# Transformer block on one core: head masks moved from K to Q, two heads' scores in one matmul, units of eight heads for the narrow token tiles

## The chip, the cores and the metric

The kernel runs on one core of a Trainium2 chip. The metric is device time in microseconds of one execution, the median of several runs; lower is better. The profile is one execution recorded by the hardware profiler. Its span runs from the first to the last instruction; the execution's own time is a little longer.

## The reference, cut to what matters

```python
x = A_x                                   # (1, 2048, 512), bf16
h = layernorm(x) * (1 + ca) + sa          # sa, ca, ga, sb, cb, gb from silu(c) @ w_mod
q, k, v = split(h @ wqkv)                 # 32 heads of 16 columns
p = softmax(q @ k.T * 16 ** -0.5)         # per head, 2048 x 2048
x = x + ga * (concat(p @ v) @ wo)
h = layernorm(x) * (1 + cb) + sb
x = x + gb * ((gelu(h @ w_gate) * (h @ w_up)) @ w_down)     # width 1792
```

Each head has only 16 columns, so the 32 x 2048 x 2048 exponentials weigh more than the matmuls.

## The kernel before, in words

**Layout.** Q and K lie transposed: 128 partitions hold a chunk of eight heads, and there are four chunks (`dc`). A row group of 32 partitions (`j`) holds two heads, an even and an odd one. A score matmul contracts over the 32 partitions of one row group, so one of its operands must have the other head's 16 rows at zero. Before, that is K: it is kept twice, `kme` with the odd heads zeroed and `kmo` with the even ones, written from one projection by two passes with a mask column each (`side_k`, L786 to L794). Q is kept once, scaled (`side_q`, L796). V is kept with a column of ones per head (`vaug`), so that the product with the exponentials also gives the softmax's denominator.

**Sets, units, rounds, banks.** Tokens of Q are worked in seven sets (`SETS`, L29): two of 512 tokens, three of 256 and two of 128. A unit is one set and one `qd` from 0 to 7, which means four heads, one in each row group: the even or the odd heads of chunk `qd // 2`. For `qd` 0 and 1 the last two sets share a unit of 256 tokens. Scores go into PSUM banks of 512 columns (`ps_sc`). A bank holds one head's scores of 512 / W key tiles for W tokens, and takes as many matmuls (`qk`, L1559): one for W = 512, two for 256, four for 128. A round is four banks, one for each head of the unit. A unit has 16 rounds at W = 512, 8 at 256 and 4 at 128. A *position* is one bank in the order of the work; there are 2048, and sets 5 and 6 begin at position 1792. PSUM has eight banks: six for scores (and now and then side work), `ps_pv` for the running products with V, and `ps_mi` for side work.

**Exponentials.** ScalarE (ACT) takes two or three banks in one exp (L403) and writes bf16 into the ring `E`. VectorE (DVE) takes some banks: from each bank a pass to an integer with the exponent in its upper bits (`bits`, L1329), and for every *quad* (the four banks of one round) three passes over 2048 columns, `mant`, `square` and `expo` (L1600 to L1614), which give two bf16 factors whose sum of products replaces the exponential. A quad holds two of ten buffers (`bufs`, L552) while it lasts. Two of these buffers are also the staging room of streamed feed-forward weights: `spare` (L1587) keeps quads out of them from shortly before the first feed-forward on, to the end (`closing`, L1450). A round may become a quad only if it is not one of its unit's last three (`cand`, L1291, with `LAST = 3`), and if it is still far enough ahead (`ahead`).

**End of a unit.** `unit_end` (L1629) copies the sums out of `ps_pv`, sends the denominators through two small DRAM scratch tensors to spread them over partitions, takes reciprocals, broadcasts them back by four DMAs, and multiplies into `onorm`. For a few late units (`PEN`, L34) it uses 32 x 32 transposes on DVE instead of the DMAs.

**Side work.** Projections, the output projection, layer norm and the feed-forward of finished sets run beside attention in small steps that a planner issues. The feed-forward of sets 0 to 3 streams its weights through staging buffers; that of sets 4 to 6 uses weights that are resident by then (`weight_parts`, L923): gate weights in Q's memory of finished tokens, down weights in `xs`, up weights in the staging buffers and a weight region. Ten parts are loaded early, from 8 positions after the end of set 3, and eleven after set 3's feed-forward. Side matmuls are split into four of 32 output rows each, so that they run in the same mode as the products with V; those of set 4's gate and up projections are kept whole, in groups of four (`WUP`, `JOIN`, L63).

**Order.** `stream` (L1242) writes the whole program at build time. At each step it looks at its own model of the engines' free times and chooses among scores, products with V, side work and filler matmuls (which keep PE's activity up). `RULES` (L73) gives nine thresholds of that choice for each stretch of 64 positions: among them `back` (backlog of DVE steps), `fill` (wanted PE activity) and `ahead`. Each engine executes its instructions in the order written; SP issues nearly all DMAs.

Of the kernel before, what the change touches and what calls it, by code (L numbers as in the profile page):

```python
# [7 lines left out]
ALU = mybir.AluOpType  # L8
# [25 lines left out]
PEN = {NSET - 2: (6, 7), NSET - 1: (5, 6, 7)}  # L34
# [18 lines left out]
def WIN(ends):  # L53
# [9 lines left out]
WUP, WDOWN, WWO, JOIN = (4,), (), (), 4  # L63
# [442 lines left out]
class _Kernel(_Recorder):  # L506
# [12 lines left out]
    def alloc(self):  # L519
        sb, ps = self.sb, self.ps  # L520
        self.xs = sb("xs", [P, NT, D], BF16)
        self.qT = sb("qT", [P, NDC, S_TOK], BF16)
        self.km = [sb("kme", [P, NDC, S_TOK], BF16), sb("kmo", [P, NDC, S_TOK], BF16)]
# [22 lines left out]
        self.wg = [self.qT[:, :, 256 * i:256 * i + 256] for i in range(6)]  # L546
        self.wg.append(hreg[:, NFC * 256:NFC * 256 + 1024].rearrange("p (a n) -> p a n", a=NDC))
        self.wu = [self.wst[i // 2][i % 2] for i in range(4)]
        self.wu += [dreg[:, 1024 * i:1024 * i + 1024].rearrange("p (a n) -> p a n", a=NDC) for i in range(4, 7)]
# [43 lines left out]
    def prologue(self):  # L593
# [27 lines left out]
        self.memset(pool, self.rm4, 1.0)  # L621
# [3 lines left out]
        self.ts(dve, self.rm[:, 0:1], self.rm[:, 1:2], -1.0, 1.0, ALU.mult, ALU.add)  # L625
# [39 lines left out]
        qb = [self.scp[:, 0, 0:256], self.scp[:, 1, 0:256]]  # L665
# [10 lines left out]
        self.act(self.km[0][:, 0, ks[0]], kb[0], ACT.Copy, scale=self.rm[:, 0:1])  # L676
        self.ts(dve, self.qT[:, 0, 0:256], qb[0], Q_SCALE, None, ALU.mult)
        self.act(self.qT[:, 0, 256:512], qb[1], ACT.Copy, scale=Q_SCALE)
        for i, h in ((0, 1), (1, 0), (1, 1)):
            self.ts(dve, self.km[i][:, 0, ks[h]], kb[h], self.rm[:, i:i + 1], None, ALU.mult)  # L680
# [61 lines left out]
    def proj(self, bank, col, g):  # L742
        for dci in range(NDC):
            self.mm(bank, self.wqkv[:, dci, col:col + P], self.hT[:, dci, 512 * g:512 * g + 512],
                    start=(dci == 0), stop=(dci == NDC - 1))
# [1106 lines left out]
```

## Time and profile before

| | |
|---|---|
| median of 3 runs | 816.21 us (816.03 to 817.04) |
| profiled execution | 815.63 us |
| its span | 813.9 us, 29942 instructions |
| DMA | 43.70 MB, mean 54 GB/s |
| granted TensorE clock | 1.000 |

In a row of groups stand: line, engine, operation, output and inputs by the program's names, output shape and input shape, count; then busy time in us and the mean duration of one in ns; then idle time of the engine just before them and who ended it. For matmuls, `32*128 32x256` means 32 contraction rows by 128 output rows, moving 256 columns. Since every operation is recorded by a helper, most lines are those of helpers: L384 is a matmul, L403 an ACT instruction, L407 a DVE product or sum of two tensors, L415 a DVE pass with a scalar, L424 a copy, L427 a reciprocal. In a row of the timeline stand the start, the length and the merged instructions with their count. In a row of waits stand who waited for whom, the total in us, the times and the longest.

### The profile page before, as it was taken

How to read it: one execution, taken by the hardware profiler on the slowest of the kernel's cores; microseconds unless marked ns; L12 is line 12 of the kernel's file. 1: busy time of each engine (PE TensorE's matmuls, PEld its weight loads, DVE VectorE, ACT ScalarE, POOL GpSimd, SP SyncE). 2: the span in 40 equal slices, each digit the busy share in tenths (PEclk: the TensorE clock that was granted, in tenths of full speed). 3: DMA queues.
4: the chain of work that ended last, by engine and by line, in shares of the span. 5: the costliest groups of instructions: out<-in, count | busy, mean ns of one | idle time of the engine just before them, and what ended most of it. 6: DMA issues, size and time to landing. Idle time of an engine off the chain costs nothing.

```text
span 813.9 us, 29942 instructions
## 1 busy us (share of the span) xinstructions
PE 749.1 (92%) x13549; PEld 301.0 (37%) x13549; DVE 753.3 (93%) x1369; ACT 792.0 (97%) x742; POOL 4.6 (1%) x13
## 2 busy tenths in 40 slices
PE   8999999888998988899998999999999999999998
PEld 3333332322222222222233333333553345456566
DVE  7877999999999999999999999999999999788675
ACT  6999999999999999999999999999999999999993
POOL 2000000000000000000000000000000000000000
PEclk9999999999999999999999999999999999999999
DMA  9100000000002211110003212100554243241000
GB/s 286 52 16 23 10 11 9 10 9 10 2 10 64 83 48 35 46 45 20 16 18 98 62 49 58 55 26 12 163 151 126 63 113 88 59 120 40 20 9 15
DMA packets 77354, 43.70 MB, mean 54 GB/s; under 512 B 21285, under 2 KB 75626, under 8 KB 77226
## 3 DMA queue, kind: packets, MB, share of 16 engines
q1 hardware_dynamic: 77224, 41.78, 18.6%
q8 instruction: 106, 1.74, 0.9%
q14 instruction: 22, 0.18, 0.1%
q10 hardware_dynamic: 2, 0.00, 0.0%
HBM read 39.15 MB, written 2.60 MB: 51 GB/s over the span
## 4 chain that ended last, share of the span: by engine, by line
ACT 84%; PE 8%; DVE 7%; DMA 0%; issue 0%; DVEq 0%
ACT E L403 80%; PE ps_sc L384 4%; ACT hreg L403 2%; PE ps_mi L384 2%; ACT L403 1%; DVE mreg L415 1%; PE ps_pv L384 1%; DVE dreg L415 1%; DVE st L446 1%; DVE mreg L407 1%; DVE hreg L415 0%; DMA xs<-in_A_x_dram 0%; DVE hreg L424 0%; PE ps_mi L388 0%; DVE mv L449 0%
## 5 line engine op out<-in xcount | busy, mean ns | idle before, releaser
L403 ACT ACTIVATE E<-ps_sc 128x1024 bf16<-128x1024 f32 (+1 forms) x701 | 746.0, 1301 | 3.0 <-PE ps_sc L384 2.8
L384 PE MATMUL ps_sc<-qT,kmo 32*128 32x256 bf16 (+2 forms) x1728 | 199.0, 294 | 23.2 <-ACT E L403 20.2
L384 PE MATMUL ps_sc<-qT,kme 32*128 32x256 bf16 (+2 forms) x1728 | 196.5, 294 | 22.0 <-ACT E L403 18.0
L415 DVE TENSOR_SCALAR mreg<-ps_sc 128x512 uint16<-128x512 f32 x256 | 171.6, 684 | 9.0 <-PE ps_sc L384 6.6
L384 PE MATMUL ps_pv<-E,vaug 128*17 128x256 bf16 (+2 forms) x2720 | 148.7, 291 | 0.2
L384 PEld LDWEIGHTS ps_sc<-qT,kme 32*128 32x128 bf16 x1728 | 57.9, 92 | 143.0 <-ACT E L403 125.5
L384 PE MATMUL ps_mi<-wreg,mreg 128*32 128x512 bf16 (+2 forms) x1792 | 106.6, 329 | 3.6 <-DVE hreg L407 1.2
L415 DVE TENSOR_SCALAR dreg<-ps_sc 128x512 uint16<-128x512 f32 x156 | 103.6, 684 | 4.9 <-PE ps_sc L384 3.6
L384 PEld LDWEIGHTS ps_sc<-qT,kmo 32*128 32x128 bf16 x1728 | 58.4, 92 | 128.8 <-ACT E L403 113.0
L384 PEld LDWEIGHTS ps_pv<-E,vaug 128*17 128x17 bf16 x2720 | 53.7, 89 | 55.6 <-issue 40.9
L415 DVE TENSOR_SCALAR mreg<-mreg 128x2048 uint16<-128x2048 uint16 x102 | 69.0, 681 | 0.1
L384 PEld LDWEIGHTS ps_mi<-wreg,mreg 128*32 128x32 bf16 (+1 forms) x1792 | 40.5, 95 | 44.0 <-issue 19.6
L384 PE MATMUL ps_pv<-mreg,vaug 128*17 128x256 bf16 (+2 forms) x848 | 50.0, 298 | 3.5 <-DVE mreg L407 1.9
L407 DVE TENSOR_TENSOR mreg<-mreg 128x2048 bf16<-128x2048 bf16 x38 | 46.1, 1214 | 0.1
L384 PE MATMUL ps_mi<-hreg,wreg 128*32 128x512 bf16 x480 | 39.5, 385 | 0.9 <-DVE qT L415 0.5
L407 DVE TENSOR_TENSOR mreg<-dreg,mreg 128x2048 bf16<-128x2048 bf16 x32 | 38.6, 1210 | 0.0
L424 DVE CAST hreg<-ps_mi 128x512 bf16<-128x512 f32 x49 | 33.6, 685 | 2.3 <-PE ps_mi L384 1.9
L384 PE MATMUL ps_mi<-wo,onorm 128*32 128x512 bf16 x416 | 31.6, 384 | 0.5 <-DVE onorm L407 0.5
L407 DVE TENSOR_TENSOR hreg<-ps_mi,hreg 128x512 bf16<-128x512 f32 x45 | 30.8, 684 | 1.3 <-PE ps_mi L384 1.0
L407 DVE TENSOR_TENSOR dreg<-mreg,dreg 128x2048 bf16<-128x2048 bf16 x26 | 31.5, 1212 | 0.0
L415 DVE TENSOR_SCALAR dreg<-dreg 128x2048 uint16<-128x2048 uint16 x46 | 31.1, 677 | 0.0
L384 PE MATMUL ps_pv<-xs,nil 128*17 128x512 bf16 (+1 forms) x464 | 30.3, 339 | 0.0
(167 smaller groups left out, 681.4 us busy)
## 6 DMA issues: line engine op xcount, KB each, us to landing
mreg<-in_B_w_up_dram SPq DMA_DIRECT2D x32, 256.0 KB, 2.9
mreg<-in_B_w_gate_dram SPq DMA_DIRECT2D x28, 256.0 KB, 3.1
mreg<-in_B_w_down_dram SPq DMA_DIRECT2D x16, 256.0 KB, 2.8
dreg<-in_B_w_down_dram SPq DMA_DIRECT2D x12, 256.0 KB, 5.3
mreg<-in_w_mod_dram SPq DMA_DIRECT2D x1, 2048.0 KB, 12.2
rb<-scr_rec SPq DMA_DIRECT2D x64, 32.0 KB, 1.9
out_dram<-xs SPq DMA_DIRECT2D x15, 128.0 KB, 1.8
rb<-scr_rec SPq DMA_DIRECT2D x104, 16.0 KB, 1.9
```

The source lines that it names most:

```text
L384: return self.rec("pe", lambda e: e.matmul(out, lhsT, rhs, start=start, stop=stop, tile_position=tp), [lhsT, rhs, *after], [out], cost=(n, ...
L403: return self.rec("act", lambda e: e.activation(out, in_, func, scale=scale, **kw), rd, wr, cost=self.cost("act", out, [in_], "act") + load)
L407: return self.rec(eng, lambda e: e.tensor_tensor(out, a, b, op), [a, b], [out], cost=self.cost(eng, out, [a, b], "tt"))
L415: return self.rec(eng, lambda e: e.tensor_scalar(out, a, s1, s2, **kw), rd, [out], cost=self.cost(eng, out, [a], "ts") + (60 if len(rd) > ...
L424: return self.rec(eng, lambda e: e.tensor_copy(out, in_), [in_], [out], cost=self.cost(eng, out, [in_], "ts"))
L446: return self.rec("dve", lambda e: e.bn_stats(out, in_), [in_], [out], cost=self.cost("dve", out, [in_], "bn"))
```

## The change: what it does, and the diff

- K is kept once (`kT`), Q twice (`qT[:, 0]` for even heads, `qT[:, 1]` for odd heads), with mask and scale in one column `rm`. A K chunk is one plain copy, a Q chunk two passes.
- From set 2 on, a unit is two `qd` (eight heads), with `n = 2`. Its score matmul has one row group of `kT` as weights and moves the even and the odd Q side by side: 2 x 256 columns for 256 tokens (one matmul per bank, not two), 2 x 128 for 128 tokens (two, not four). A bank now holds both heads' scores for half as many key tiles. The last two `qd` of set 6 stay apart (`APART`), with four heads each and four matmuls per bank.
- A unit of 256 tokens thus has 16 rounds, one of 128 tokens eight, and the joint unit 16. Products with V keep their number and width, but those of the two heads go into different columns of the one `ps_pv` bank. Before the first of a paired unit, four matmuls with zero weights clear the bank.
- `unit_end` works on the wider unit, with one chain of small DMAs for eight heads. `PEN` is set anew.
- Up weights for the resident feed-forward go into the odd half of Q's memory. Eighteen parts are loaded early (after set 1's feed-forward as well) and three late. The staging buffers are given back to quads once set 3's feed-forward is done, and only streaming feed-forwards wait for them.
- Set 4's gate and up matmuls are no longer whole (`WUP` is empty).
- 30 of the 32 rows of `RULES` have other thresholds. Three unused projection functions are removed.

```diff
-PEN = {NSET - 2: (6, 7), NSET - 1: (5, 6, 7)}
+PEN = {NSET - 2: (6,), NSET - 1: (4, 6, 7)}
+APART = {NSET - 2: (), NSET - 1: (6, 7)}
-WUP, WDOWN, WWO, JOIN = (4,), (), (), 4
+WUP, WDOWN, WWO, JOIN = (), (), (), 4
...
-        self.qT = sb("qT", [P, NDC, S_TOK], BF16)
-        self.km = [sb("kme", [P, NDC, S_TOK], BF16), sb("kmo", [P, NDC, S_TOK], BF16)]
+        self.qT = sb("qT", [P, 2, NDC, S_TOK], BF16)
+        self.kT = sb("kT", [P, NDC, S_TOK], BF16)
-        self.wg = [self.qT[:, :, 256 * i:256 * i + 256] for i in range(6)]
+        self.wg, self.wu = ([self.qT[:, x, :, 256 * i:256 * i + 256] for i in range(6)] for x in range(2))
...
         def fin(mi):
-            self.ts("dve", self.km[0][:, dc, sl], mi, self.rm[:, 0:1], None, ALU.mult)
-            self.ts("dve", self.km[1][:, dc, sl], mi, self.rm[:, 1:2], None, ALU.mult)
+            self.copy("dve", self.kT[:, dc, sl], mi)
...
         def fin(mi):
-            self.ts("dve", self.qT[:, dc, 512 * g:512 * g + 512], mi, Q_SCALE, None, ALU.mult)
+            for e in range(2):
+                self.ts("dve", self.qT[:, e, dc, 512 * g:512 * g + 512], mi, self.rm[:, e:e + 1], None, ALU.mult)
...
-        return g[:6] + d[:4], g[6:] + u + d[4:]
+        return g + u[:6] + d[6:] + d[:4], u[6:] + d[4:6]
...
-        while not self.dry and self.held & {1, 2}:
+        while flow and not self.dry and self.held & {1, 2}:
...
-        units = [((k,), qd) + SETS[k] for k in range(NSET - 2) for qd in range(8)]
-        units += [((NSET - 2, NSET - 1), qd, SETS[NSET - 2][0], 2 * P) for qd in range(QS)]
-        units += [((k,), qd) + SETS[k] for k in (NSET - 2, NSET - 1) for qd in range(QS, 8)]
+        units = [((k,), qd) + SETS[k] + (1,) for k in range(2) for qd in range(8)]
+        units += [((k,), qd, SETS[k][0], 2 * SETS[k][1], 2) for k in range(2, NSET - 2) for qd in range(0, 8, 2)]
+        units += [((NSET - 2, NSET - 1), qd, SETS[NSET - 2][0], 4 * P, 2) for qd in range(0, QS, 2)]
+        for k in (NSET - 2, NSET - 1):
+            units += [((k,), qd, SETS[k][0], 2 * P, 2) for qd in range(QS, 8, 2) if qd not in APART[k]]
+            units += [((k,), qd, SETS[k][0], P, 1) for qd in APART[k]]
...
-            if parts and pos >= loaded and (pos >= ends[FLOW - 1] + 8 if early else ("ffn", FLOW - 1) in self.have):
+            if parts and pos >= loaded and (pos >= ends[FLOW - 1] + 8 and ("ffn", 1) in self.have if early else ("ffn", FLOW - 1) in self.have):
...
-            self.closing = self.flowing or pos > ends[0] - 40
+            self.closing = (self.flowing or pos > ends[0] - 40) and ("ffn", FLOW - 1) not in self.have
...
+                if n == 1:
+                    q = self.qT[rows, qd % 2, dc, q0:q0 + C]
+                else:
+                    out, q = out.rearrange("p (e n) -> p e n", e=2), self.qT[rows, :, dc, q0:q0 + C // 2]
+                self.mm(out, self.kT[rows, dc, P * kt:P * kt + P], q, tp=(32 * j, 0))
...
+        if first and n == 2:
+            for j in range(4):
+                self.mm(acc[32 * j:32 * j + VW, 0:C], self.nil[:, 0:VW], self.xs[:, NT - 1, 0:C], True, False, (0, 32 * j))
...
-        self.copy("dve", osb, acc[:, 0:W])
+        self.copy("dve", osb, acc[:, 0:C])
```

More of the change, by code (lines that the diff above doesn't have):

```diff
@@ L1634, in unit_end, with over @@
         self.live[u] = (lo, hi)
-        m = 4 * W // P
-        o = 8 if BCOL[sets[0]] else 0
+        m, o, c = 4 * C // P, lo % 256 // 32, OCOL[sets[0]]
+        den, rden = self.den[:, b, o:o + m], self.rden[:, b, o:o + m]
+        def over():
+            if self.probing is None:
+                self.live.pop(u)
+                for k in sets:
+                    for e in range(n):
+                        self.done(("onorm", k, qd + e))
         if len(sets) == 1 and qd in PEN.get(sets[0], ()):
-            self.blocks32(osb, acc[:, 0:W])
-            k = sets[0]
+            self.blocks32(osb, acc[:, 0:C])
@@ L1649, in unit_end @@
+            self.task([lambda: self.recip(rden, part[:, :, DH]),
                        lambda: self.tt("dve", norm.rearrange("p (b r) -> p b r", r=32), part,
-                                       rec.rearrange("p (b o) -> p b o", o=1).broadcast_to([P, m, 32]), ALU.mult),
-                       back], ("onorm", k, qd))
+                                       rden.rearrange("p (b o) -> p b o", o=1).broadcast_to([P, m, 32]), ALU.mult)]
+                      + [lambda e=e: back(e) for e in range(n)], None)
```

125 lines of the change are left out of this document (48 added, 77 removed), and 60 rows, old and new, of the table RULES.

## Prediction

> **What bounds the kernel now.** I read the page first, then busy time by stage, then the forms of the groups in single stages.
>
> ```profile
> span 813.9 us, 29942 instructions
> PE 749.1 (92%) x13549; PEld 301.0 (37%) x13549; DVE 753.3 (93%) x1369; ACT 792.0 (97%) x742; POOL 4.6 (1%) x13
> ACT 84%; PE 8%; DVE 7%; DMA 0%; issue 0%; DVEq 0%
> ```
>
> ScalarE (ACT) is busy for 97% of the span and makes up 84% of the chain that ended last. What it does is exp.
>
> ```profile
> L403 ACT ACTIVATE E<-ps_sc 128x1024 bf16<-128x1024 f32 x455 | 447.1, 1160 | 0.7 <-PE ps_sc L384 0.6
> L403 ACT ACTIVATE E<-ps_sc 128x1536 bf16<-128x1536 f32 x242 | 352.7, 1579 | 0.6 <-PE ps_sc L384 0.6
> ```
>
> Count in banks of 512 scores: 455x2 + 242x3 = 1636 on ACT. The whole attention has 32 heads x 16 key tiles x 2048 / 512 = 2048 banks, so VectorE (DVE) exponentiates the other 412. One bank more in an exp lengthens it by 1579 - 1160 = 419 ns: I use **0.42 us of ACT per bank**. What a bank costs DVE:
>
> ```profile
> L415 DVE TENSOR_SCALAR mreg<-ps_sc 128x512 uint16<-128x512 f32 x256 | 171.6, 684 | 9.0 <-PE ps_sc L384 6.6
> L415 DVE TENSOR_SCALAR dreg<-ps_sc 128x512 uint16<-128x512 f32 x156 | 103.6, 684 | 4.9 <-PE ps_sc L384 3.6
> L415 DVE TENSOR_SCALAR mreg<-mreg 128x2048 uint16<-128x2048 uint16 x102 | 69.0, 681 | 0.1
> L407 DVE TENSOR_TENSOR mreg<-mreg 128x2048 bf16<-128x2048 bf16 x38 | 46.1, 1214 | 0.1
> ```
>
> 256 + 156 = 412 is the count above. Each bank takes 684 ns, and each quad of four banks two integer passes of 681 and a product of 1214: 684 + (681 + 1214 + 681) / 4 = **1.33 us of DVE per bank**. Moving a bank to DVE also shortens the stage by 0.42 us, in which DVE then has less room, so it needs 1.33 + 0.42 = 1.75 us of DVE time. **The exchange rate: 1 us of DVE time made free and used gives 0.42 / 1.75 = 0.24 us.** The rate holds only where ACT is full. Stages, with the late ones apart:
>
> ```profile
> core 0: us, PE busy (x) PEld busy (x) DVE busy (x) ACT busy (x) POOL busy (x), PEclk, DMA share, GB/s
> 60.00:170.00 110.00, 100.93 (x1850) 36.58 (x1846) 102.03 (x165) 109.97 (x102) 0.00 (x0) 1.00 0.06 13
> 170.00:305.00 135.00, 120.46 (x1464) 33.26 (x1461) 133.38 (x218) 135.00 (x129) 0.00 (x0) 1.00 0.12 34
> 500.00:600.00 100.00, 95.52 (x2025) 40.87 (x2023) 97.76 (x175) 99.95 (x92) 0.00 (x0) 1.00 0.26 72
> 600.00:700.00 100.00, 94.03 (x2122) 43.94 (x2110) 98.52 (x174) 99.95 (x94) 0.00 (x0) 1.00 0.38 104
> 700.00:790.00 90.00, 88.04 (x2183) 52.19 (x2175) 70.11 (x151) 89.88 (x88) 0.00 (x0) 1.00 0.19 46
> 790.00:814.00 24.00, 20.11 (x359) 15.17 (x356) 14.22 (x43) 10.42 (x15) 0.00 (x0) 1.00 0.05 15
> ```
>
> The columns after the stretch are its length and the busy time of each engine. ACT has no idle time from 60 to 790. DVE is full too (98%), except before 170 (8.0 us idle) and **from 700 to 790: 19.9 us idle**. That is the stage of the 128-token tiles. Its groups show the same loss as a lower DVE share; first 600 to 700, then 700 to 790:
>
> ```profile
> L415 DVE TENSOR_SCALAR mreg<-ps_sc 128x512 uint16<-128x512 f32 x38 | 25.3, 684 | 0.7 <-PE ps_sc L384 0.2
> L415 DVE TENSOR_SCALAR dreg<-ps_sc 128x512 uint16<-128x512 f32 x20 | 13.1, 682 | 0.4 <-PE ps_sc L384 0.3
> ```
>
> ```profile
> L415 DVE TENSOR_SCALAR dreg<-ps_sc 128x512 uint16<-128x512 f32 x16 | 10.6, 684 | 2.4 <-PE ps_sc L384 2.3
> L415 DVE TENSOR_SCALAR mreg<-ps_sc 128x512 uint16<-128x512 f32 x12 | 8.3, 688 | 2.0 <-PE ps_sc L384 1.8
> ```
>
> 58 banks per 100 us go to DVE in the first, 28 in 90 us in the second.
>
> **The change part by part.**
>
> *Scores in one matmul.* Scores are 1728 + 1728 = 3456 matmuls now:
>
> ```profile
> L384 PE MATMUL ps_sc<-qT,kmo 32*128 32x256 bf16 (+2 forms) x1728 | 199.0, 294 | 23.2 <-ACT E L403 20.2
> L384 PE MATMUL ps_sc<-qT,kme 32*128 32x256 bf16 (+2 forms) x1728 | 196.5, 294 | 22.0 <-ACT E L403 18.0
> ```
>
> Afterwards: 1024 for sets 0 and 1, 768 for sets 2 to 4, 64 for the joint unit, 192 + 128 for the pairs of sets 5 and 6, 128 for the two single units: 2304. But a trio of banks takes PE no longer in many matmuls than in few, since three row groups run side by side:
>
> ```profile
> 667.51 0.39 PE L384 MATMUL ps_sc<-qT,kme 32*128 32x256 bf16 x6
> 717.44 0.40 PE L384 MATMUL ps_sc<-qT,kmo 32*128 32x128 bf16 x12
> 719.18 0.45 PE L384 MATMUL ps_sc<-qT,kmo 32*128 32x128 bf16 x12
> ```
>
> Six of 256 columns take 0.39 us, and twelve of 128 take 0.40 or 0.45 us. And PE has slack, for it runs matmuls that are only filler:
>
> ```profile
> L384 PE MATMUL ps_pv<-xs,nil 128*17 128x512 bf16 (+1 forms) x464 | 30.3, 339 | 0.0
> L384 PE MATMUL ps_mi<-xs,ident 128*32 128x512 bf16 (+1 forms) x184 | 15.3, 379 | 0.1
> ```
>
> So I cost the 1152 matmuls fewer at 0 on the path. Bounds: if PE had no slack, each of the last stage's 88 ACT instructions at most, with one trio each, would gain 0.06 us (0.45 - 0.39), or 5 us; and no loss, as the columns are the same. The 72 or so added zeroing matmuls (4 for each paired unit) are of the filler's kind, about 0.07 us each (30.3 / 464): 5 us of PE, under the 45.6 us of filler above: 0.
>
> *Q and K.* The masks cost a pass each, and move from K to Q:
>
> ```profile
> L415 DVE TENSOR_SCALAR kme<-ps_mi,rm x15: 742/750/752, 25.6 to 156.7; 128x512 bf16<-128x512 f32 x15
> L415 DVE TENSOR_SCALAR kmo<-ps_mi,rm x15: 741/742/744, 26.3 to 157.4; 128x512 bf16<-128x512 f32 x15
> L415 DVE TENSOR_SCALAR qT<-ps_mi x15: 678/682/692, 59.7 to 221.7; 128x512 bf16<-128x512 f32 x15
> ```
>
> Per chunk 750 + 742 + 682 becomes one plain pass (682) and two masked ones (750 + 742): the same sum. Only the place differs: K ends at 157 us, Q at 222. About four Q chunks lie past 170, where DVE is full, and each takes 0.8 us more there: 3.2 us x 0.24 = **+0.8 us**; what K gives back falls before 170, where DVE has room, so I give it 0 (bounds: 0 to 2). In the prologue passes are exchanged one for one: 0.
>
> *Units of eight heads.* Each unit ends with a copy, a reciprocal and a product on DVE. For 256 and for 512 columns:
>
> ```profile
> L424 DVE COPY osb<-ps_pv 128x256 f32<-128x256 f32 x26 | 10.8, 416 | 0.5 <-PE ps_pv L384 0.3
> L407 DVE TENSOR_TENSOR onorm<-osb,rb 128x256 bf16<-128x256 f32 x26 | 10.8, 417 | 0.0
> L427 DVE RECIPROCAL rden<-den 128x8 f32<-128x8 f32 x26 | 5.0, 194 | 0.0
> L424 DVE COPY osb<-ps_pv 128x512 f32<-128x512 f32 x15 | 10.2, 683 | 0.2 <-PE ps_pv L384 0.2
> L407 DVE TENSOR_TENSOR onorm<-osb,rb 128x512 bf16<-128x512 f32 x16 | 10.9, 684 | 0.0
> L427 DVE RECIPROCAL rden<-den 128x16 f32<-128x16 f32 x16 | 3.9, 244 | 0.0
> ```
>
> Two ends of 256 cost 2 x (416 + 417 + 194) = 2.05 us, one of 512 costs 1.61: a merger saves 0.44 us. There are 18: twelve in sets 2 to 4, one joint, five in sets 5 and 6. The twelve, in a full stage, save 5.3 us: x 0.24 = **-1.3 us**. The other six save 2.6 us in the stage that has DVE time over, counted next (their ends are of 128 and 256 columns or go by transposes, with prices from 0 to the same 0.44). SP issues seven DMAs less for each merger that isn't of the transposing kind; SP isn't waited for: 0.
>
> *The longer unit also changes who may go to DVE.* A quad may only be one of a unit's rounds that is not among its last three. A 128-token unit has four rounds, so one in four qualifies: 12 of the 48 in sets 5 and 6, and 7 quads (28 banks) were started from 700 on. A 256-column unit of eight rounds has five, a 512-column unit of sixteen 13. Afterwards sets 5 and 6 have 5 pairs x 5 + 2 x 1 = 27 of 48, about the share (5 of 8) with which DVE is 98.5% busy from 600 to 700. **This is the main term.** If DVE reached that level, 19.9 - 1.3 = 18.6 us would be used, with the 2.6 us above 21.2. Bounds: 0 (the planner starts no more quads) and 21.2 x 0.24 = 5.1. I take the 18.6, by the row of 600 to 700, and nothing for the 2.6: **-4.5 us**.
>
> *Up weights in Q's room.* Eighteen transfers instead of ten go early, one per 8 positions from about 588 us on, and three instead of eleven late. SP's queue carries them past the small DMAs of the unit ends. In the trace the late ones were in time: ACT ran on through 700 to 790. So 0, from -1 to +1. What it leaves behind is the staging room, open again to quads once the feed-forward of set 3 is done: ten buffers for the last stage, not eight. Eight were enough for 98.5% from 600 to 700, so this only secures the term above. The rows of the search table I can't price: 0, from -2 to +2.
>
> *Up matmuls of set 4 no longer whole.* 112 matmuls over 128 columns become 448 over 32, 336 more, in the last stage. Four split ones run side by side, so columns cost the same: 0; the price without cover is a rival below.
>
> Sum: -1.3 - 4.5 + 0.8 = **-5.0 us**. The profiled execution took 815.63 (span 813.9 and 1.7 around it), which gives 810.6; the median of the runs is 0.6 above it, so I forecast **811.2**.
>
> **A rule against it.** The row: ACT 792.0 us (97%), and no part of this change makes an exp shorter. The Trainium skill, Perfetto Trace Analysis, section Identifying the Most-Contended Engine, says to take the engine with the highest occupancy first. By it a change of PE's and DVE's work leaves the time as it is, unless it moves exps off ACT; that is the second rival.
>
> **The rivals.**
>
> *More.* DVE also fills the 8.0 us before 170 (x 0.24 = 1.9), takes all 21.2 (5.1), loses nothing on Q, and the 24 us after 790, with ACT only 10.42 busy, shrink by a tenth (2.4): 1.3 + 5.1 + 1.9 + 2.4 = 10.7, or **805.5**. For it: ACT never waits, so each bank counts. Against: before 170 the limit is the projections' order, which stays.
>
> *Nothing.* The freed DVE time turns to idle, since DVE in the last stage waits in order for PE results of the feed-forward, and the quads don't rise; only -1.3 + 0.8 is left: **815.7**. For it: these waits, of 700 to 790.
>
> ```profile
> DVE wreg L407 <- PE ps_mi L384: 3.2, 2, 2.2
> DVE xs L407 <- PE ps_sc L384: 2.4, 2, 1.7
> DVE osb L431 <- PE ps_pv L384: 2.2, 1, 2.2
> ```
>
> Against: together 7.8 us of 19.9.
>
> *Slower.* The 336 added matmuls of set 4's feed-forward make PE late. The densest row is
>
> ```profile
> 770.00:780.00 10.00, 9.57 (x332) 5.87 (x332) 8.20 (x23) 10.00 (x11) 0.00 (x0) 1.00 0.05 7
> ```
>
> or 30 ns a matmul, so 336 cost PE 10.1 us between about 720 and 760. Filler and shorter score bursts can hide perhaps half; 5 us reach ACT as waits, DVE gains nothing there, and with -1.3 + 0.8 the time is **820.7**; with three quarters hidden, 818.2. It decides once the rate would exceed 332 per 10 us; 700 to 790 has 2183, or 243 per 10 us, and four tens with 84 more each come to 327: just below. The Trainium skill, Runtime: NRT & Kernel Launch, section Instruction fetch mechanics, says that crossing a block of 256 instructions is mostly hidden; by that rule this rival costs nothing. No row here isolates it.
>
> **How the numbers follow.** Forecast (807.5 to 814.5) 0.58; more (below 807.5) 0.16; nothing (814.6 to 817.8) 0.11; slower 0.15. A difference of 0.2%, 1.6 us, is about what a measurement can tell. Faster 0.74, same 0.11, slower 0.15. The range runs from 804.5, a little under the price of more, to 818.5, the mild slower case.
>
> **What would show it.** Right: DVE above 90% and some 40 banks instead of 28 on DVE in the last 90 us of exps, or 11 to 14 banks more than 412 on DVE in all; 18 unit ends fewer; ACT still without idle. Score matmuls 2304. Wrong: DVE still near 78% late (nothing), ACT waiting for PE on scores after 720 (slower), or a DVE share that falls between 170 and 230 by more than three banks.

## The result and the profile after

The changed kernel takes **814.62 us** (median of 12 runs, 814.23 to 816.0), and on the same chips the kernel before takes 816.59 (12 runs, 815.49 to 818.14): a ratio of 0.9975 [0.9966, 0.9984], or 2.0 us faster. Forecast were 5.0. Measured again on another chip, the two kernels lie 1.6 us apart (run e13 below). One execution of run e5 below took 937.1 us at a granted clock of 0.65 and is left out of its figure. The profiled execution of the changed kernel took 814.79 us. Its page, with the lines that answer to those of before:

```profile
span 813.1 us, 28154 instructions
PE 749.0 (92%) x12749; PEld 289.8 (36%) x12749; DVE 759.8 (93%) x1330; ACT 789.1 (97%) x741; POOL 4.6 (1%) x13
ACT 66%; PE 20%; DVE 12%; issue 1%; DMA 0%; DVEq 0%
```

All lines of the code stand one lower now (L385 is a matmul, L404 an ACT instruction, L416 a DVE pass with a scalar). ACT's busy time fell by 2.9 us, DVE's rose by 6.5. In the chain that ended last, ACT fell from 84% to 66%, and PE rose from 8% to 20%. The groups with their forms kept apart, on ACT and DVE:

```profile
L404 ACT ACTIVATE E<-ps_sc 128x1024 bf16<-128x1024 f32 x460 | 452.4, 1151 | 1.5 <-PE ps_sc L385 1.2
L404 ACT ACTIVATE E<-ps_sc 128x1536 bf16<-128x1536 f32 x236 | 344.6, 1582 | 1.2 <-PE ps_sc L385 1.1
L416 DVE TENSOR_SCALAR mreg<-ps_sc 128x512 uint16<-128x512 f32 x288 | 192.4, 685 | 12.6 <-PE ps_sc L385 10.2
L416 DVE TENSOR_SCALAR dreg<-ps_sc 128x512 uint16<-128x512 f32 x132 | 88.3, 686 | 2.1 <-PE ps_sc L385 1.1
L408 DVE TENSOR_TENSOR onorm<-osb,rb 128x512 bf16<-128x512 f32 x29 | 19.8, 684 | 0.0
L425 DVE COPY osb<-ps_pv 128x512 f32<-128x512 f32 x28 | 19.1, 683 | 0.0
```

DVE takes 288 + 132 = 420 banks instead of 412, so ACT has eight fewer: 8 x 0.42 = 3.4 us. The wide ends are there too (28 copies of 512 columns instead of 15, three of 256 instead of 26). The stages in which before lost time or had DVE idle:

```profile
60.00:170.00 110.00, 101.11 (x1856) 36.33 (x1855) 104.87 (x172) 108.67 (x103) 0.00 (x0) 1.00 0.06 13
600.00:700.00 100.00, 95.20 (x1878) 43.13 (x1874) 97.65 (x161) 99.89 (x93) 0.00 (x0) 1.00 0.43 124
700.00:790.00 90.00, 87.50 (x2258) 46.47 (x2250) 77.46 (x148) 89.69 (x89) 0.00 (x0) 1.00 0.09 24
790.00:814.00 24.00, 19.23 (x307) 14.73 (x304) 13.15 (x39) 8.89 (x14) 0.00 (x0) 1.00 0.04 13
```

DVE's 70.11 us between 700 and 790 became 77.46: a little over a third of its 19.9 us of idle time was used, not nearly all of it. Its banks in that stretch:

```profile
L416 DVE TENSOR_SCALAR mreg<-ps_sc 128x512 uint16<-128x512 f32 x31 | 21.1, 688 | 6.3 <-PE ps_sc L385 5.8
L416 DVE TENSOR_SCALAR dreg<-ps_sc 128x512 uint16<-128x512 f32 x4 | 2.6, 684 | 0.4 <-PE ps_sc L385 0.4
```

That is 35 banks, not 28, and DVE now waits 6.2 us for scores before it takes them (4.1 before). Where the last exp ends is seen on ACT's timeline, at the load of gelu's table for set 6. Before, then after:

```profile
793.60 1.28 ACT L403 ACT_TABLE_LOAD   x1
```

```profile
792.08 1.28 ACT L404 ACT_TABLE_LOAD   x1
```

And the chain alone from 686 us on, by line, before and then after:

```profile
by line: ACT E L403 57.9%; PE ps_sc L384 16.7%; PE ps_mi L384 6.8%; PE ps_pv L384 4.1%; ACT hreg L403 2.5%; ACT L403 2.0%; DVE mreg L407 0.9%; DVE E L415 0.8%; DVE hreg L407 0.8%; issue 0.6%; DVE wreg L407 0.6%; DVE dreg L415 0.5%; DVE st L
```

```profile
by line: PE ps_sc L385 43.8%; PE ps_mi L385 18.9%; PE ps_pv L385 11.8%; DVE mreg L416 4.0%; DVE dreg L416 1.9%; ACT E L404 1.8%; DVE hreg L425 1.5%; DVE osb L425 1.1%; DVE st L447 1.0%; DVE mreg L408 1.0%; issue 0.9%; DVE hreg L416 0.9%; DV
```

The exps held 57.9% of this stretch and hold 1.8% now, although ACT is still busy for 89.69 of the 90 us from 700 to 790, and PE for 87.50. A chain names only the engine that came last at each step, so with two engines as full as these it flips on little. It doesn't say that ACT has room.

**Where the time went.** Adding up the 512-column banks of ACT's exps and of DVE's integer passes in order of time gives the moment at which a position is reached. Position 512 (end of set 0) comes at 207.9 us before and 208.5 after, 1024 (end of set 1) at 394.3 and 395.4, 1792 (sets 5 and 6 begin) at 686.3 and 686.8. From there to the last exp it takes 107.3 and 105.3, and to the end of the span another 20.3 and 21.0. So sets 0 and 1 lose 1.1, sets 2 to 4 gain 0.6, the *late stage* (from position 1792 to the last exp) gains 2.0, and the end loses 0.7. That sums to 0.8 between the two spans. DVE's banks from position 1792 on, called *late banks* below, are 35 before and 40 after. Repeats show how firm these moments are: the runs e9 and e14, which are the kernel before up to position 1792, reach 1024 at 394.6 and 394.5, and e13, the changed kernel, at 395.1. So the loss in sets 0 and 1 lies between 0.5 and 1.1; the 0.6 of sets 2 to 4 is the same in all of them. The medians differ by 2.0; the profiled execution of before lies 1.0 under its median of the 12 runs, that of after 0.2 above, and about 1 us of the gain is thus not to be seen in these two traces.

### The profile page after: what moved, and what is told of

The parts are those of the page before. It is cut to its first block, busy times and chain, and to the rows that moved or that the text cites. A ratio compares the mean times of both kernels' runs of the same rounds, so it can differ in the third digit from the quotient of the medians.

```text
span 813.1 us, 28154 instructions
## 1 busy us (share of the span) xinstructions
PE 749.0 (92%) x12749; PEld 289.8 (36%) x12749; DVE 759.8 (93%) x1330; ACT 789.1 (97%) x741; POOL 4.6 (1%) x13
## 4 chain that ended last, share of the span: by engine, by line
ACT 66%; PE 20%; DVE 12%; issue 1%; DMA 0%; DVEq 0%
ACT E L404 63%; PE ps_sc L385 10%; PE ps_mi L385 7%; DVE mreg L416 4%; PE ps_pv L385 3%; ACT hreg L404 2%; DVE dreg L416 1%; ACT L404 1%; DVE dreg L408 1%; DVE hreg L425 1%; DVE mreg L408 1%; DVE st L447 1%; DVE hreg L408 0%; DVE osb L425 0%; DVE wreg L408 0%
## 5 line engine op out<-in xcount | busy, mean ns | idle before, releaser
L404 ACT ACTIVATE E<-ps_sc 128x1024 bf16<-128x1024 f32 (+1 forms) x700 | 743.0, 1293 | 4.3 <-PE ps_sc L385 3.9
L385 PE MATMUL ps_sc<-qT,kT 32*128 32x512 bf16 (+2 forms) x2304 | 281.2, 360 | 43.8 <-ACT E L404 37.3
L416 DVE TENSOR_SCALAR mreg<-ps_sc 128x512 uint16<-128x512 f32 x288 | 192.4, 685 | 12.6 <-PE ps_sc L385 10.2
L385 PEld LDWEIGHTS ps_sc<-qT,kT 32*128 32x128 bf16 x2304 | 73.0, 91 | 271.5 <-ACT E L404 227.7
L385 PE MATMUL ps_pv<-E,vaug 128*17 128x256 bf16 (+2 forms) x2696 | 149.2, 292 | 0.1
L385 PE MATMUL ps_mi<-wreg,mreg 128*32 128x512 bf16 (+1 forms) x1760 | 102.0, 330 | 5.1 <-DVE hreg L408 1.9
L416 DVE TENSOR_SCALAR dreg<-ps_sc 128x512 uint16<-128x512 f32 x132 | 88.3, 686 | 2.1 <-PE ps_sc L385 1.1
L416 DVE TENSOR_SCALAR mreg<-mreg 128x2048 uint16<-128x2048 uint16 x113 | 76.5, 683 | 0.3
L385 PEld LDWEIGHTS ps_pv<-E,vaug 128*17 128x17 bf16 x2696 | 54.7, 90 | 59.1 <-issue 43.8
L385 PEld LDWEIGHTS ps_mi<-wreg,mreg 128*32 128x32 bf16 x1760 | 38.5, 95 | 45.0 <-issue 18.1
L385 PE MATMUL ps_pv<-mreg,vaug 128*17 128x256 bf16 (+2 forms) x900 | 49.5, 292 | 1.1 <-DVE mreg L416 0.5
L385 PE MATMUL ps_pv<-xs,nil 128*17 128x512 bf16 (+1 forms) x584 | 48.4, 375 | 1.1 <-DVE osb L425 1.1
L385 PE MATMUL ps_mi<-hreg,wreg 128*32 128x512 bf16 (+1 forms) x484 | 39.6, 384 | 2.9 <-DVE qT L416 1.6
L425 DVE CAST hreg<-ps_mi 128x512 bf16<-128x512 f32 (+1 forms) x50 | 33.7, 674 | 3.4 <-PE ps_mi L385 2.6
L385 PE MATMUL ps_mi<-wo,onorm 128*32 128x512 bf16 x448 | 33.5, 383 | 0.1
L416 DVE TENSOR_SCALAR dreg<-dreg 128x2048 uint16<-128x2048 uint16 x42 | 28.5, 679 | 0.0
L385 PE MATMUL ps_mi<-mreg,hreg 128*32 128x512 bf16 x352 | 28.3, 385 | 0.0
L385 PE MATMUL ps_pv<-dreg,vaug 128*17 128x256 bf16 (+2 forms) x468 | 27.3, 296 | 0.4 <-DVE dreg L408 0.2
```

Of the source, the lines that this page charges most:

```text
L385: return self.rec("pe", lambda e: e.matmul(out, lhsT, rhs, start=start, stop=stop, tile_position=tp), [lhsT, rhs, *after], [out], cost=(n, ...
L404: return self.rec("act", lambda e: e.activation(out, in_, func, scale=scale, **kw), rd, wr, cost=self.cost("act", out, [in_], "act") + load)
L416: return self.rec(eng, lambda e: e.tensor_scalar(out, a, s1, s2, **kw), rd, [out], cost=self.cost(eng, out, [a], "ts") + (60 if len(rd) > ...
L425: return self.rec(eng, lambda e: e.tensor_copy(out, in_), [in_], [out], cost=self.cost(eng, out, [in_], "ts"))
```

## The experiments

**Theories.** The prediction let the longer units raise DVE's late share, because more rounds of a unit may become quads (theory U). Against it: the share follows the planner's thresholds in `RULES` (theory T), or the staging room given back (theory R). Then there is the question why more banks on DVE bring so little time. Ratios are to the kernel before on the same chip.

**1. The table.** e1 is the changed kernel with the old table, e2 the old kernel with the new one, e3 the old kernel in which three of the four rounds of a 128-token unit may become quads, and nothing else.

```diff
 RULES = (                                             # e1: all rows old again; e2 the other way round
     (60, 200, 7, 3900, 1536, 500, 1600, 24, 700),
-    (80, 50, 10, 4200, 1536, 1100, 2500, 20, 700),
+    (80, 50, 10, 4200, 1536, 400, 1600, 20, 3200),
...
-LASTW = {}                                            # e3
+LASTW = {128: 1}
```

> The kernel after, with the threshold table of the kernel before and nothing else changed. Theory T (the late VectorE share follows the planner's thresholds): from 700 to 790 us VectorE falls back to about 28 banks and under 72 us busy, as before the change, and the time is 819 to 823. Theory U (it follows the unit's length, as the prediction had it): it keeps 35 banks or more and some 77 us busy there, and the time stays within 2 us of 814.6.

> The kernel before, with the threshold table of the kernel after and nothing else changed. Theory T: from 700 to 790 us VectorE rises to about 35 banks although the units still have four rounds; elsewhere the thresholds fit the order badly, so the time is 819 to 826. Theory U: 28 banks or fewer there, as in the kernel before.

> The kernel before, where three of the four rounds of a 128-token unit may become quads instead of one. Theory U, in its own words (one round in four qualifies, that is what holds VectorE back late): 35 banks or more from 700 to 790 us, and at least 1.5 us faster than before. Theories T and S (something else holds it back): 28 banks, give or take 3, and no gain; up to 3 us slower from the disturbed order.

Measured: e1 820.58 (1.0056 [1.0041, 1.0071]), e2 825.8 (1.012 [1.0102, 1.0138]), e3 818.75 (1.0037 [1.0022, 1.0053]). All three are slower. DVE's banks between 700 and 790, of e1, e2 and e3:

```profile
L416 DVE TENSOR_SCALAR mreg<-ps_sc 128x512 uint16<-128x512 f32 x16 | 11.0, 686 | 2.3 <-PE ps_sc L385 2.1
L416 DVE TENSOR_SCALAR dreg<-ps_sc 128x512 uint16<-128x512 f32 x12 | 8.1, 689 | 4.4 <-PE ps_sc L385 4.0
```

```profile
L415 DVE TENSOR_SCALAR mreg<-ps_sc 128x512 uint16<-128x512 f32 x26 | 17.5, 684 | 5.0 <-PE ps_sc L384 4.9
L415 DVE TENSOR_SCALAR dreg<-ps_sc 128x512 uint16<-128x512 f32 x12 | 8.2, 688 | 5.0 <-PE ps_sc L384 4.9
```

```profile
L415 DVE TENSOR_SCALAR mreg<-ps_sc 128x512 uint16<-128x512 f32 x20 | 13.6, 688 | 4.2 <-PE ps_sc L384 4.1
L415 DVE TENSOR_SCALAR dreg<-ps_sc 128x512 uint16<-128x512 f32 x8 | 5.4, 685 | 1.6 <-PE ps_sc L384 1.5
```

Long units with the old table: 28 banks, as before. Short units with the new table: 38. More candidate rounds: 28. But e1 and e2 reach position 1792 only at 689.8 and 692.2, so a fixed stretch doesn't hold the same work. Counted in late banks, before has 35, e1 28, e2 39 and e3 35. **U falls, T holds** for the banks: with the old table, long units have even fewer late banks than short ones. The time is another matter. Each structure with the other's table is slower as a whole, by 4.6 and 9.8 us (the ratios on 816.6), and e2's exps from position 1792 on take 108.4 us in spite of 39 banks, against 107.3 before.

**2. The ladder of the structure, all with the old table.** e5: K once, Q twice and masked (the lines of the change shown above), units of four heads. e6: e5 and units of eight heads, with the new `PEN` and `APART`. e7: e6 and the up weights in Q's room, with the early loads and the staging buffers given back. e1 above is e7 with set 4's matmuls split. e16 is e5 once more, for its profile.

```diff
-        units = [((k,), qd) + SETS[k] + (1,) for k in range(NSET - 2) for qd in range(8)]      # e5 -> e6
+        units += [((k,), qd, SETS[k][0], 2 * SETS[k][1], 2) for k in range(2, NSET - 2) for qd in range(0, 8, 2)]
-        return g[:6] + d[:4], g[6:] + u + d[4:]                                               # e6 -> e7
+        return g + u[:6] + d[6:] + d[:4], u[6:] + d[4:6]
-WUP, WDOWN, WWO, JOIN = (4,), (), (), 4                                                       # e7 -> e1
+WUP, WDOWN, WWO, JOIN = (), (), (), 4
```

> First step from the kernel before towards the kernel after, with the old threshold table throughout: only the masks move to Q, units keep four heads, nothing else. Theory Q (the change has one physical cost, the second Q pass on VectorE before 222 us, more than the 0.8 us of the prediction): this step alone is 3 to 5 us slower than before, and the delay has built up by the end of set 1 (about 394 us). Theory F (each step costs because the thresholds were set for another order, whatever the step contains): 1 to 3 us slower, and the later steps e6, e7 and e1 each move the time by 1 to 4 us in either direction. By the prediction's own sum: 0.8 slower.

> Second step: e5 and units of eight heads, with the old table. By the prediction's sum 1.3 to 5.8 us faster than e5, with VectorE at 35 banks or more from 700 to 790 us. Theory T (the late VectorE share follows the thresholds): about 28 banks there, as e1 showed; then the saved unit ends are the only gain, at most 1.9 us (7.9 us of VectorE x 0.24). Theory F: slower than e5 by 1 to 4 us in spite of the saved unit ends.

> Third step: e6 and the up weights in Q's room, the early loads and the two buffers given back, with the old table; up matmuls of set 4 still whole. The prediction's sum: within 1 us of e6. Between this kernel and e1 lies only the splitting of set 4's up matmuls: if the slower rival's mechanism is at work (336 more matmuls make TensorE late), this kernel is 2 us or more faster than e1's 820.6; else within 1 us of it.

> The kernel of e5 again, for its profile. The second Q pass costs what falls up to 394 us, the end of set 1: 1 to 2 us there (after has 1.1, e6 1.7), with 3 to 5 banks fewer on VectorE by then. Theory F: the other 4 us of e5's loss lie behind that, where neither Q nor K is written any more.

Measured: e5 822.4 (1.0072 [1.005, 1.0093]), e16 822.75 (1.008 [1.0062, 1.0098]), e6 823.07 (1.0086 [1.007, 1.0102]), e7 821.1 (1.0058 [1.004, 1.0076]). The first step costs some 6 us. Of these, e16 has lost 3.6 by position 1024 (397.9 against 394.3, a part of it by a lower clock, see the end), 5.4 by 1792, and 8.2 at the last exp, with 33 late banks. e6 has the same Q and K code and a full clock up to there: it has lost 1.7 by position 1024, and DVE has taken 203 banks by then, before 207. Four banks at 0.42 us are 1.7, inside the prediction's bounds for the masks (0 to 2). Most of e5's loss lies behind that, where neither Q nor K is written, and why it grows there isn't shown; thresholds that were found for one order of work and don't fit another would explain it. Eight heads add nothing under the old table (26 banks on DVE between 700 and 790 in e6, 28 late banks), the room gives about 2 back, and the split is neutral there, as far as intervals of some 1.5 us to either side can tell (e7 against e1: 1.0058 and 1.0056).

**3. Single parts of the change undone, with the new table.** e10 keeps set 4's gate and up matmuls whole, e11 has the up weights in their old place, loads them late and keeps the two staging buffers closed to quads, e12 has four-head units in sets 5 and 6 and in their joint units, with the old `PEN`.

```diff
-WUP, WDOWN, WWO, JOIN = (), (), (), 4                                        # e10
+WUP, WDOWN, WWO, JOIN = (4,), (), (), 4
-        return g + u[:6] + d[6:] + d[:4], u[6:] + d[4:6]                      # e11
+        return g[:6] + d[:4], g[6:] + u + d[4:]
-            units += [((k,), qd, SETS[k][0], 2 * P, 2) for qd in range(QS, 8, 2) if qd not in APART[k]]   # e12
+        units += [((k,), qd) + SETS[k] + (1,) for k in (NSET - 2, NSET - 1) for qd in range(QS, 8)]
```

> The kernel after with set 4's gate and up matmuls whole again (112 over all columns of the array instead of 448 over a quarter each). If splitting them costs TensorE time, as the prediction's slower rival had it: 1 to 4 us faster than after. If it saves time (no change of mode between these and the products with V, finer steps for the planner): 1 to 4 us slower, with ScalarE waiting for scores between 720 and 760 us. By the prediction's sum: no difference.

> The kernel after with the up weights in their old place: late loads, and the two staging buffers closed to quads to the end. The prediction's sum gave this part 0, from -1 to +1. Theory R (the two buffers feed the late stage): 1 to 3 us slower than after, with 36 banks or fewer on VectorE after 686 us. Else within 1 us, and 39 to 41 banks.

> The kernel after with units of four heads for the last two sets alone (score matmuls of 128 columns and four to a bank there, shared unit of 256 columns), the new table kept. Theory U (long units raise VectorE's late share): 35 banks or fewer after 686 us. Theory T: 38 to 42 banks all the same, and the time differs from after only by the disturbed order: 815 to 820.

Measured: e10 816.78 (1.0009 [1.0, 1.0019]), e11 814.97 (0.9987 [0.9978, 0.9996]), e12 817.74 (1.002 [1.0011, 1.003]). All three have 40 late banks, as the changed kernel has. So with the new table neither the room (R falls) nor the unit length sets the share. e12 is slower by some 3 us all the same, and e10 by 2 to 3, each with a table that was made for the other form; which part of it is the form's own isn't settled. But **the split that the slower rival feared shows no cost in the time**. On PE it costs a little: for set 4's gate and up products 96 whole matmuls of 256 columns keep PE busy for 7.3 + 7.0 us in e10, and the 384 split ones in their place for 8.3 + 7.9 us in the changed kernel. ACT waits no more between 720 and 760 in e10 than in the changed kernel (busy for 39.59 and 39.89 of 40 us, where waits were expected). In e10 the last exp ends at 791.8, even earlier (792.1 in the changed kernel); the time is lost behind it, 23.4 us instead of 21.0, where PE still has side work:

```profile
790.00:814.00 24.00, 21.44 (x347) 16.48 (x343) 16.30 (x43) 8.60 (x14) 0.00 (x0) 1.00 0.03 10
```

PE is busy for 21.44 us there and DVE for 16.30, against 19.23 and 13.15.

**4. More banks for DVE.** From position 1792 on, side work may borrow a second score bank when its credit exceeds a threshold of the table; a step then has two banks for ACT and none for DVE. e4 lends less often. e8 is e4 and leaves out the whole feed-forward of set 4 (its 256 tokens are written without it): its time isn't that of the full work.

```diff
-                self.two = self.fifth or (pos >= TWO_AT(ends) and self.credit > self.rule.side2)               # e4, e8
+                self.two = self.fifth or (pos >= TWO_AT(ends) and self.credit > max(3600, self.rule.side2))
+        if gi == 4 and not begin:                                                                              # e8
+            for t in tiles:
+                self.dma("sp", self.out[0, P * t:P * t + P, :], self.xs[:, t, :], "out%d" % (t % 4))
+            yield END
+            return
```

> The kernel after, where side work takes the sixth score bank as its second bank only when it is far behind (credit above 3600 instead of the table's 700 to 3200). Theory S (in the last stage side work holds the bank that a VectorE exp would need): 42 banks or more on VectorE from 700 us to the last exp, fewer exps of two banks without one on VectorE, the last exp at least 2 us earlier, but side work left over for the end, so that the whole takes 815 to 821. Without S: VectorE's banks stay at about 35 from 700 to 790.

> The kernel of e4 (after, second side bank only when far behind), and the whole feed-forward of set 4 left out: its 256 tokens are written without it. It is a probe of what fills the last stage. Theory S with P (the stage from 690 us is full because side work takes a bank and TensorE's time from the scores): VectorE takes 50 banks or more after 690 us, ScalarE's waits for scores of e4 (86.1 us busy of 90) shrink to under 1.5 us, and the last exp comes 6 us or more before that of e4. If VectorE is held by its own order of work, it stays at about 40 to 48 banks and only the feed-forward's ScalarE and VectorE passes (5.9 us of ScalarE) come off.

Measured: e4 818.97 (1.0038 [1.0023, 1.0053]), e8 805.33 (0.9868 [0.9847, 0.9889]). e4 has 48 late banks instead of 40, but its last exp ends at 792.1, as in the changed kernel (at least 2 us earlier were expected), and 25.8 us follow it instead of 21.0. Its row of 700 to 790, and ACT's waits there:

```profile
700.00:790.00 90.00, 84.77 (x2406) 45.97 (x2405) 82.64 (x152) 86.11 (x79) 0.00 (x0) 1.00 0.09 24
```

```profile
L404 ACT ACTIVATE E<-ps_sc 128x1024 bf16<-128x1024 f32 x49 | 47.8, 1065 | 1.5 <-PE ps_sc L385 1.4
L404 ACT ACTIVATE E<-ps_sc 128x1536 bf16<-128x1536 f32 x26 | 37.5, 1510 | 2.4 <-PE ps_sc L385 2.3
```

DVE is at 92% here, the level that the prediction had hoped for; and now ACT has idle time, waits for PE's scores, and side work piles up behind the last exp. It isn't PE's time as a whole that runs out. Filler from 686 to 792 takes 9.9 us in e4, 5.3 in the changed kernel and 3.5 before (in the first two it holds a few matmuls that clear a bank), and PE is idle there for 6.1, 2.7 and 2.0 us. The largest group of filler in e4:

```profile
L385 PE MATMUL ps_pv<-xs,nil 128*17 128x256 bf16 x180 | 7.7, 274 | 0.4 <-DVE osb L425 0.4
```

So PE had time for both and used it for neither. What e4 takes away is the second bank of side work, and side work is what falls behind; why ACT's scores come late beside that much filler isn't shown.

With e8's side work gone, the last exp ends at 782.5, 9.5 us earlier than in e4, with the same 48 banks (at least 50 were expected), and ACT's waits for scores fall from 3.7 to 1.4 us. But 5.9 of the 9.5 is work of ACT itself that e8 leaves out, two gelus and two of the three table loads; these rows are e4's from 686 us on:

```profile
L404 ACT ACT_TABLE_LOAD x3 | 3.8, 1283 | 0.0
L404 ACT ACTIVATE hreg<-hreg 128x1792 bf16<-128x1792 bf16 x2 | 3.3, 1690 | 0.0
```

At most some 3.6 us are what the lighter load of PE and its banks gave the exps, and 4.4 more come from the shorter end (21.3 against 25.8). The chain from 686 us on goes back to ACT in e8:

```profile
by line: ACT E L404 48.9%; PE ps_sc L385 17.0%; PE ps_mi L385 11.8%; PE ps_pv L385 6.3%; issue 1.2%; DVE E L416 0.8%; DVE wreg L408 0.6%; DVE st L447 0.6%; DVE hreg L425 0.5%; DVE onorm L408 0.5%; DVE nwt L421 0.4%; DVE osb L425 0.3%; DVE r
```

**5. Only the last four rows of the table**, those for positions from 1792 on: the old kernel with the new ones (e9, again as e14), the changed kernel with the old ones (e15), and the changed kernel beside them on the same chip (e13).

```diff
-    (80, 300, 6, 3900, 3500, 500, 2500, 16, 2500),
-    (80, 50, 10, 4200, 2048, 650, 1900, 20, 1800),
-    (80, 50, 9, 3900, 3500, 0, 1900, 20, 1800),
-    (60, 50, 11, 4200, 3500, 300, 1900, 20, 1800),
+    (80, 450, 8, 3900, 3500, 500, 2500, 16, 2500),
+    (80, 50, 13, 4200, 2048, 650, 1900, 20, 1800),
+    (60, 50, 9, 3900, 3500, 1500, 1900, 24, 3200),
+    (60, 50, 11, 3900, 3500, 300, 1900, 20, 1800),
```

> The kernel before with only the last four rows of the threshold table (positions 1792 to 2047, from about 686 us on) taken from the kernel after; no other line differs. Theory T in its sharpest form (the whole gain comes from late thresholds that let VectorE take more banks, and the new structure isn't needed for it): the course up to 686 us is as before, VectorE takes 38 banks or more from there on instead of 35, and the time is 813.5 to 815.5, as fast as the kernel after. If the units of eight heads are needed for the late gain: 816 or slower, and 35 banks or fewer.

> The kernel after, unchanged, so that it stands on the same chip as the next two. 0.9975 of before, as measured, give or take 0.001.

> The kernel of e9 (before, with the last four rows of the new table), unchanged. If the new structure brings nothing that these rows do not, it is within 0.1% of e13. If it does, it is 1 us or more slower than e13, which e9's ratio of 0.9994 points to; then the profile must show where: in the end after the last exp (22.1 us in e9, 21.0 in after) or in the exps.

> The kernel after with the old last four rows of the table: the mirror of e9. Theory T: VectorE's banks after 686 us fall from 40 to 37 or fewer, the last exp comes 1 to 2 us later than in after, and the time is 815.5 to 817, level with before. If long units keep the gain: 39 banks or more, and within 0.5 us of e13.

Measured: e9 815.45 (0.9994 [0.9985, 1.0003]); on one chip e13 814.76 (0.9984 [0.9975, 0.9993]), e14 815.15 (0.9986 [0.9977, 0.9995]) and e15 814.99 (0.9985 [0.9976, 0.9994]). On that chip four rows on the old structure bring 1.2 of the 1.6 us that 32 rows and the new structure bring, and the intervals of e14 and e13 overlap; e9, the same kernel on another chip, gained less (0.9994). The bank counts went as T has it: 43 late banks in e9 and e14, 36 in e15, where DVE is busy for 72.96 us between 700 and 790. Yet e15, with four banks fewer than e13 and its last exp 1.3 us later (793.0 against 791.7), takes the same time, where T expected 815.5 to 817: T explains the banks and not the time.

The runs in order of late banks, in us of their profiled executions (banks and the position 1792 counted as above; e13 repeats the changed kernel's row and e9 that of e14, within 0.2):

| kernel | late banks | 1792 to last exp | last exp to end | both |
|---|---|---|---|---|
| e6 old table, eight heads | 28 | 111.8 | 20.7 | 132.5 |
| e7 old table, room | 28 | 110.2 | 19.7 | 129.8 |
| e1 new, old table | 28 | 109.6 | 20.1 | 129.7 |
| e16 old table, Q masks | 33 | 110.1 | 19.7 | 129.8 |
| e3 old, more rounds | 35 | 108.6 | 21.3 | 129.9 |
| before | 35 | 107.3 | 20.3 | 127.6 |
| e15 new, old four rows | 36 | 106.5 | 20.0 | 126.5 |
| e2 old, new table | 39 | 108.4 | 21.9 | 130.3 |
| after | 40 | 105.3 | 21.0 | 126.3 |
| e11 new, old room | 40 | 105.0 | 21.8 | 126.7 |
| e12 new, late four heads | 40 | 106.2 | 23.0 | 129.2 |
| e10 new, whole matmuls | 40 | 104.7 | 23.4 | 128.1 |
| e14 old, new four rows | 43 | 104.6 | 22.3 | 126.8 |
| e4 new, one side bank | 48 | 104.8 | 25.8 | 130.5 |

From before to after, five banks shorten the exps by 2.0 us, or 0.40 a bank; from after to e4, eight banks shorten them by 0.5, and what comes behind grows by 4.8. The count alone sets neither column: e2's exps take 108.4 with 39 banks, and the four kernels with 40 banks differ by up to 1.6 in the exps and 2.9 in the sum. No version here that does the whole work clearly beats the changed kernel.

## Why the prediction was wrong

**The step that failed is the main term**, -4.5 us: "If DVE reached that level, 19.9 - 1.3 = 18.6 us would be used", taken as reached because longer units let more rounds become quads. The late stage gained 2.0 us instead.

- *The cause.* Longer units don't raise the share by themselves (e1: 28 late banks, before 35), and more candidate rounds don't either (e3: 35). The thresholds move it (e2: 39; e9: 43; e15: 36 against 40). The rows of the table, which the prediction could not price and took at 0 from -2 to +2, hold the gain: without them the changed kernel is 4.6 us slower than before, not 2.0 faster. It doesn't hang on the last four rows alone, since e15 keeps the time without them.
- *The amount.* DVE used 7.35 us more between 700 and 790, not 18.6, and took five late banks more, not ten or eleven (18.6 / 1.75). By the prediction's own signs: 86% of that stretch and not above 90, 35 banks and not some 40, eight banks more in all and not 11 to 14. DVE waits in order for PE's scores, 6.2 us in that stretch, and a part of the rounds has no bank for DVE, since side work holds one (e4 lends less often and has 48 late banks).
- *The rate* held as far as the change went: 0.40 us of exp a bank, where the prediction had 0.42. It doesn't hold up to the level that the prediction took: e4 has DVE at 92%, and its last exp ends no earlier than with eight banks fewer. The prediction gave PE slack because it runs 45.6 us of filler, but that row is of the whole span. In the late stage (686 to 792) the kernel before had 3.5, with PE busy for 103.98 of 106 us; its two larger groups there:

```profile
L384 PE MATMUL ps_mi<-xs,ident 128*32 128x512 bf16 x28 | 2.6, 387 | 0.0
L384 PE MATMUL ps_sc<-xs,ident 128*32 128x512 bf16 x4 | 0.4, 390 | 0.2 <-ACT E L403 0.2
```

  That is little cover, but e4 with its 9.9 us of filler shows that lack of PE time isn't what ends the gain there. What does, beside the bank that side work has to do without, stays open.
- *The end.* The forecast left the time behind the last exp as it was; it grew by 0.7 us, and by 4.8 more in e4.

The other steps:

- **The exchange for sets 2 to 4**, -1.3: measured -0.6. The ends became cheaper as worked out (29 products of 512 columns at 684 ns). DVE has two banks more there (172, and 170 before), where 5.3 us / 1.75 gives three. The 0.6 lies between the prices of one bank and two, so about half of the term came.
- **Q masks**, +0.8 past 170 us: 0.5 to 1.1 lost by position 1024, the size about right and the place wrong. ACT's idle time rose by 1.3 us between 60 and 170, where the prediction had DVE with room; DVE's banks by 1024 didn't fall (208, and 207 before). No run holds the masks alone against the new thresholds; with the old ones they cost 1.7 by there (e6). ACT's waits from 20 to 175 us, before and after:

```profile
ACT E L403 <- PE ps_sc L384: 0.6, 1, 0.6
```

```profile
ACT E L404 <- PE ps_sc L385: 1.7, 3, 0.8
```

- **Score matmuls** at 0: there are 2304, as counted, and 0 was right. All score matmuls together keep PE busy for 281.2 us, and for 282.9 before.
- **Up weights in Q's room** at 0, from -1 to +1: right under the new table (e11, within 1 us, and 40 late banks without the room). Under the old one it was worth about 2 (e7 against e6).
- **Nothing** was the rival nearest to the measured time (815.7), with the reason that DVE waits in order for PE. That half was right; but the banks did rise.
- **Slower** had the price wrong. It took 10.1 us of PE for the 336 added matmuls; the 288 of them counted above cost 1.9 (16.2 against 14.3 us). In the time they show no cost (e7 and e1, 1.0058 and 1.0056), and under the new table the whole ones go with the slower kernel (e10). The Trainium skill, Runtime: NRT & Kernel Launch, section Instruction fetch mechanics, says that crossing a block of instructions is mostly hidden; e1 with 28040 instructions against e7 with 27350 agrees.
- **The rule against the change** (the engine with the highest occupancy first) named ACT, and what was gained did come with eight banks off ACT. The page Perfetto Trace Analysis of the Trainium skill says in its section Optimization Strategy that the most contended engine may differ between regimes of one kernel. By the chain this trace agrees: after the change ACT holds 66% of the whole span, and PE's scores alone hold 43.8% from 686 us on. By occupancy it doesn't: ACT is still the fullest engine from 700 to 790, with 89.69 us against PE's 87.50.

## What to carry to other kernels

Take cover from the stage in which it is needed: 45.6 us of filler in a span were 3.5 in the stage that mattered. When work is moved off a full engine, price how much the other engine will really take, not only what each piece brings: here the rate was right and the amount half of what was hoped. Look also behind the stage, since what it gains can come back there: filling DVE to 92% made the kernel slower. A change that comes with a retuned table needs the crossed runs (new code with old table, old code with new table, only the rows of one stage): here four rows on the old code brought most of what the whole change did.

## What the runs showed that was not expected

- **Four matmuls over 32 output columns side by side cost PE hardly more than one over 128**: 0.169 us for four against 0.149 for one, at 256 columns (16.2 us / 96 in the changed kernel, 14.3 / 96 in e10). In the time no cost is seen beside products with V that are split the same way: 821.1 whole (e7) and 820.58 split (e1), though it is 336 matmuls more.
- **The granted clock isn't always full on a single busy core.** Some executions have one short dip to half. In e16 it lies between 94 and 98 us, and the averages of 5 us show it:

```profile
85.00:90.00 5.00, 4.72 (x63) 1.27 (x59) 4.62 (x10) 5.00 (x7) 0.00 (x0) 1.00 0.07 17
90.00:95.00 5.00, 4.59 (x76) 2.09 (x72) 4.22 (x8) 4.82 (x5) 0.00 (x0) 0.91 0.00 0
95.00:100.00 5.00, 4.59 (x48) 0.89 (x44) 4.02 (x8) 4.03 (x5) 0.00 (x0) 0.75 0.02 5
100.00:105.00 5.00, 4.63 (x116) 1.91 (x112) 4.78 (x8) 5.00 (x5) 0.00 (x0) 1.00 0.03 7
```

The mean from 94 to 98 us is 0.57, and the two single microseconds from 95 to 97 stand at 0.50. The profiles of e1 and e7 have the same dip at the same place (0.57 from 93 to 97 us, and 0.51 from 93 to 100). Its cause isn't shown. The runs of one kernel show what it goes with: of e13's eleven, the three with a mean clock of 0.998 took 815.67 to 815.99 us, the eight others 814.28 to 815.2.
